# Matrix memory in steps of 64 tokens instead of 128, as 64x64 tiles of the array

## The chip, the cores and the metric

The kernel runs on one core of one Trainium2 chip. The time is the device time of one execution, in microseconds; three runs of the kernel before took 416.53, 416.6 and 417.84 us, so its median is 416.6 us. Profiles come from one further profiled execution. Engines are named as in the profile: PE is TensorE (matrix products; PEld its weight loads), DVE is VectorE, ACT is ScalarE, POOL is GpSimd, SP is SyncE, which issues the loads and stores.

## The reference

Two blocks follow each other. The first is a matrix-memory LSTM cell over q, k, v of shape 4 batches x 8 heads x 768 tokens x 40, with an input, a forget and an output gate:

```
m_new  = max(f[t] + m, i[t])
f_stab = exp(f[t] + m - m_new);  i_stab = exp(i[t] - m_new)
C = f_stab * C + i_stab * outer(v[t], k[t])        # 40 x 40 per head
n = f_stab * n + i_stab * k[t]
y[t] = sigmoid(o[t]) * (C q[t]) / max(|n . q[t]|, 1)
```

The heads are then put side by side (320 features a token). The second block takes the real part of a two-dimensional Fourier transform over tokens and features, adds it to its input, normalizes each token, and runs an MLP 320 -> 1280 -> 320 with a ReLU and a residual. All of it is float32.

## The kernel before

**The recurrence in chunks.** The 768 tokens of a batch are cut into NT = 6 chunks of L = 128. A chunk's output has two parts. One comes from the state C that entered the chunk: `mlstm_from_state` multiplies C by the queries, which `mlstm_scale_q` has scaled by their decay (`qg`). The other comes from the chunk itself: `mlstm_scores` makes k by q products (`ps`), `mlstm_exp` on ACT makes the weights W from the spread gate maxima, `mlstm_mask` on POOL zeroes the later tokens (batch 0 has the mask in its spread maxima), `mlstm_weigh` on DVE multiplies `ps` into W, and `mlstm_from_chunk` multiplies W by the values. Both parts add up in the PSUM tile `ph`. The values have a column of ones, so that n rides along as column 41 (D1).

The state goes on by `mlstm_to_state`: k times the weighted values `vw` (made by `mlstm_scale_v` on POOL) into `pc`. `mlstm_decay` on POOL multiplies the old state by the chunk's decay. In batch 0 the decayed state is added to `pc` by an identity product (L501) and ACT copies `pc` out (L511); in batches 1 to 3 DVE adds it (L515).

**Tiles of the array today.** Two heads share one set of operands. Scores (L465): two row tiles of 64 rows (40 in use) by 128 columns. State products (L479): C is block diagonal, two heads in one 128x128 product. Values (L486) and products to the state (L496): two column tiles, 128 rows by 64 columns. A score tile is the full 128x128 square, of which the upper triangle is used.

**After the products.** `mlstm_gather` (ACT) copies `ph` to `hT`, partly backwards, and moves the first column of a chunk to its neighbour; `mlstm_turn` transposes on TensorE into `px`; `mlstm_finish` (DVE, five operations, L549 to L555) divides, applies the output gate and writes x.

**Order.** There is no scheduler at work: `at(slot, phase, fn)` puts every piece of work into a plan by hand, and it is issued in that order on each engine's queue. Within a slot the phases are EVAC, FILL, MAIN and FILL_PE. Slots 0 to 31 have batch 0's recurrence, its Fourier products and the conversion of the MLP weights on DVE (`Piece`: the lines 344 to 364). From slot 31 on each slot has one step of some batch's MLP as MAIN, and the next batch's recurrence, one chunk each three slots, in FILL and FILL_PE around it: batch 1's from slot 32, batch 2's from 50, batch 3's from 82. The MLP's products are L861, L852 and L986 for batch 0, L923, L928 and L1042 for the others.

The PSUM pools: `ps_s` two banks (scores), `ps_h` two buffers of one bank shared by `ph`, `pc`, `px` and early transposes, `ps_m` four banks for everything else.

Of the kernel before, what the change touches and what calls it, by code (L numbers as in the profile page):

```python
# [19 lines left out]
L = 128  # L20
NT = S // L
NP = H // 2
D1 = D + 1
# [27 lines left out]
def kernel(  # L51
# [28 lines left out]
    ps_h = pool("ps_h", 2, space=PSUM)  # L80
    ps_m = pool("ps_m", 1, space=PSUM)

    turn = iter("3210321032120312031230123012012301023130201320132013201320123021320321")
# [11 lines left out]
    later_b = const.tile([L, L], BF, name="later_b")  # L95
    spread_sb = const.tile([BH, L + BH // 2], FP, name="spread_sb")
    colT = const.tile([L, NT, 2, BH], FP, name="colT")
    decB = const.tile([L, BH // 2, NT], FP, name="decB")
# [11 lines left out]
    C_bufs = [const.tile([L, NP, L], FP, name=f"C{n}") for n in range(3)]  # L110
# [3 lines left out]
    Cd_bufs = [s_last[:, n * NP * D1:(n + 1) * NP * D1].rearrange("p (n m) -> p n m", m=D1) for n in range(2)]  # L114
    hT_bufs = [const.tile([L, NP, L], FP, name=f"h{n}") for n in range(2)]
    M_d = dram.tile([NT, BH, L], FP, name="M_d")
    G_d = dram.tile([NT, 2, BH // 2, L], FP, name="G_d")
# [16 lines left out]
    def idle_products(n, first=False):  # L134
        pw = bank("pi", [L, 2 * L]) if first else ps_s.tile([L, 2 * L], FP, name="pi", tag="ps")
        for i in range(n):
            nc.tensor.matmul(pw, rest[:, 0:L], rest, start=True, stop=True, skip_group_check=True)


    def gates(gp):  # L140
        f_sb = gp.tile([BH, NT, L], FP, name="f_sb")
        a = gp.tile([BH, NT, L], FP, name="a")
        nc.sync.dma_start(out=f_sb.rearrange("p c t -> p (c t)"), in_=f_gate.rearrange("b h s -> (b h) s"))
        nc.sync.dma_start(out=a.rearrange("p c t -> p (c t)"), in_=i_gate.rearrange("b h s -> (b h) s"))
        keep = gp.tile([BH, NT, L], FP, name="keep")
        shift = gp.tile([BH, NT, L], FP, name="shift")
        m_in = gp.tile([BH, NT, 1], FP, name="m_in")
        F = gp.tile([BH, NT, L], FP, name="F")
        M = gp.tile([L, NT, L], FP, name="M")
        wk = gp.tile([BH, NT, L], FP, name="wk")  # L150
        g = gp.tile([L, NT, L], FP, name="g")
        nM = gp.tile([BH, NT], FP, name="nM")
        M3 = gp.tile([3 * BH, NT, L], BF, name="M3")
        below = gp.tile([BH, NT, L], BF, name="below")
        sel = gp.tile([3 * BH, BH], BF, name="sel")
        nc.vector.memset(rest, 0.0)
# [7 lines left out]
        nc.gpsimd.affine_select(out=later_b, in_=later_b, compare_op=OP.is_ge, fill=-M_INIT, base=0, pattern=[[1, L]],  # L164
                                channel_multiplier=-1)
# [6 lines left out]
        nc.vector.memset(M[:, 0:2], 0.0)  # L172
        for t in C_bufs:
            nc.scalar.copy(out=t.rearrange("p (two n) t -> p two (n t)", two=2),
                           in_=rest.unsqueeze(1).to_broadcast([L, 2, 2 * L]))
        nc.gpsimd.memset(qk_bufs[1][:, 0], 0.0)
        mlstm_load_o(0, 0)
        mlstm_load(0, 1)
        nc.gpsimd.memset(qk_bufs[2][:, 0], 0.0)
# [4 lines left out]
        for t in hT_bufs + Cd_bufs:  # L184
            nc.gpsimd.memset(t, 0.0)
# [8 lines left out]
        def maxima(s, initial):  # L194
            c0, c1 = s.start, s.stop
            nc.vector.tensor_tensor(out=a[:, s], in0=a[:, s], in1=F[:, s], op=OP.subtract)
            if c0 > 0:
                nc.vector.tensor_copy(out=shift[:, s, 0:1], in_=F[:, c0 - 1:c1 - 1, L - 1:L])
            nc.vector.tensor_tensor_scan(out=flat(M, s), data0=flat(shift, s), data1=flat(a, s), initial=initial,
                                         op0=OP.add, op1=OP.max)  # L200
            nc.vector.tensor_scalar(out=nM[:, s], in0=M[0:BH, s, L - 1], scalar1=-1.0, scalar2=None, op0=OP.mult)
            if c0 > 0:
                nc.vector.tensor_tensor(out=m_in[:, s], in0=M[0:BH, c0 - 1:c1 - 1, L - 1:L],
                                        in1=F[:, c0 - 1:c1 - 1, L - 1:L], op=OP.add)

        def spread_max(b, c, h0):

            k = chunks[b, c]
            if h0 == 0:
                k.W = wp.tile([L, H, L], FP, name="W", tag="W")  # L210
                k.M = []
            k.M.append(bank("pM", [L, NP, L]))
            nc.tensor.matmul(k.M[-1], ident_b, later_b.unsqueeze(1).to_broadcast([L, NP, L]), start=True, stop=False,
                             skip_group_check=True)
            for h in range(h0, h0 + NP):
                bh = b * H + h
                w, x = (ident[:, bh:bh + 1], M[:, c, :]) if c < 2 else (sel[:, bh:bh + 1], M3[:, c, :])
                nc.tensor.matmul(k.M[-1][:, h - h0, :], w.to_broadcast([w.shape[0], L]), x, start=False, stop=True,
                                 skip_group_check=True)
# [10 lines left out]
        def spread_decay(b, c):  # L230
            k = chunks[b, c]
            k.G = bank("pG", [L, NP, L])
            for h in range(H):
                r, bh = slice(h % 2 * 64, (h % 2 + 1) * 64), b * H + h
                nc.tensor.matmul(k.G[r, h // 2, :], ident[:, bh:bh + 1].to_broadcast([L, 64]), g[:, c, :],
                                 start=True, stop=True)

        def weights(s):
            for c in range(s.start, s.stop):
                nc.scalar.activation(out=wk[:, c], in_=a[:, c], func=AF.Exp, bias=nM[:, c:c + 1])  # L240
# [5 lines left out]
        def columns(s, j):  # L246
            pt = ps_h.tile([L, NT, BH], FP, name="pt", tag="ph")
            for c in range(s.start, s.stop):
                nc.tensor.transpose(pt[:, c, :], (a, wk)[j][:, c, :], ident[0:BH, 0:BH])
            return pt  # L250

        first, others, last = slice(0, 1), slice(1, NT), slice(2, NT)
        sums(first)
        maxima(first, M_INIT)
        pt = columns(first, 0)
        nc.scalar.copy(out=colT[:, first, 0], in_=pt[:, first])
        weights(first)
        spread_max(0, 0, 0)
        pt = columns(first, 1)
        spread_max(0, 0, NP)  # L260
# [3 lines left out]
        nc.vector.tensor_copy(out=colT[:, first, 1], in_=pt[:, first])  # L264
        mlstm_exp(0, 0, NP)
        maxima(others, M[0:BH, 0, L - 1:L])
        pt = columns(others, 0)
        mlstm_load_o(0, 1)
        nc.vector.memset(g[:, 1:3], 0.0)
        nc.vector.tensor_copy(out=colT[:, others, 0], in_=pt[:, others])  # L270
        decay(slice(1, 2))
        weights(others)
        spread_max(0, 1, 0)
        spread_max(0, 1, NP)
        spread_decay(0, 1)
        pt = columns(others, 1)
        late = {"pt": pt}
# [4 lines left out]

        def columns_late():
            nc.vector.tensor_copy(out=colT[:, others, 1], in_=late["pt"][:, others])

        def decay_late():
            decay(last)
            for hip in range(2):
                nc.sync.dma_start(out=G_d[1:NT, hip].rearrange("c p t -> p c t"), in_=g[hip:BH:2, 1:NT])

        def decays():
            dec = gp.tile([BH, BH // 2, NT], FP, name="dec")
            nc.vector.tensor_tensor(out=dec[:, :, 1:],
                                    in0=g[0:BH, 1:, L - 1].unsqueeze(1).to_broadcast([BH, BH // 2, NT - 1]),
# [983 lines left out]
```

## Time and profile before

| | |
|---|---|
| median of 3 runs | 416.6 us |
| profiled execution, first to last instruction (its span) | 414.0 us |
| median over this span | 2.6 us |
| granted TensorE clock | 1.000 |
| instructions | 8020 |
| PE, DVE, ACT, POOL busy | 404.0, 289.3, 188.8, 115.7 us |
| moved by DMA | 47.14 MB, mean 114 GB/s |
| first product of the MLP starts at | 57.4 us |

The page gives no time for the profiled execution other than its span; the 2.6 us are taken to lie around it. A float32 product stands in the trace as two weight loads and two products (`x16` in the chain is eight products). [...] In the rows of windows the columns are the stretch, its length, the busy time of PE, PEld, DVE, ACT and POOL with the number of instructions, the granted clock, the DMA engines' share and GB/s.

### The profile page before, as it was taken

The page shows a single profiled execution, that of the slowest core. Times are in us where ns is not written, and L with a number is a line of the kernel's source. Part 1 is how long each engine was busy: PE and PEld are TensorE (multiplying, and loading weights), DVE is VectorE, ACT ScalarE, POOL GpSimd, SP SyncE. Part 2 cuts the span into 40 slices and gives each one's busy share as a digit, 9 for nine tenths or more (in the row PEclk, how much of TensorE's full clock was granted, in tenths as well). Part 3 has the DMA queues.
Part 4 walks back from the last instruction along what each step waited for, and adds up shares of the span by engine and source line. Part 5 has one row for each costly group of instructions (what it writes and reads, how often), then busy time and mean ns, then how long its engine had stood idle before and what let it go on. Part 6 is the DMA issues. An engine that isn't in the chain of part 4 may idle for free.

```text
span 414.0 us, 8020 instructions
## 1 busy us (share of the span) xinstructions
PE 404.0 (98%) x2966; PEld 304.2 (73%) x2966; DVE 289.3 (70%) x682; ACT 188.8 (46%) x493; POOL 115.7 (28%) x194
## 2 busy tenths in 40 slices
PE   8999999999999999999999999999999999999997
PEld 6877555666667778776559998976559988555996
DVE  8789894978885548777874569787863786335652
ACT  6986366686651232655455413745551113355000
POOL 5554201567442420342061430342040000020000
PEclk9999999999999999999999999999999999999999
DMA  7899298479564154266100544310000000000010
GB/s 227 291 251 334 71 275 265 132 223 289 187 193 148 61 153 143 63 213 205 45 0 2 156 152 132 95 50 1 0 2 0 33 32 34 0 0 2 22 43 32
DMA packets 20549, 47.14 MB, mean 114 GB/s; under 512 B 2784, under 2 KB 9312, under 8 KB 20384
## 3 DMA queue, kind: packets, MB, share of 16 engines
q1 hardware_dynamic: 20512, 46.65, 36.6%
q8 instruction: 23, 0.38, 0.4%
q14 instruction: 14, 0.11, 0.1%
HBM read 42.52 MB, written 4.11 MB: 113 GB/s over the span
## 4 chain that ended last, share of the span: by engine, by line
PE 88%; DVE 8%; ACT 2%; POOL 1%; issue 1%; ACTq 0%; DVEq 0%
PE po L1042 18%; PE pm L923 17%; PE po L986 8%; PE pm L928 6%; PE ph L486 5%; PE pm L861 5%; PE ps L465 5%; PE ph L479 4%; PE pu L740 3%; PE px L540 2%; PE pm L852 2%; PE pz L709 2%; PE put L783 2%; PE pc L496 1%; PE pz L697 1%; DVE stats L767 1%
## 5 line engine op out<-in xcount | busy, mean ns | idle before, releaser
L992 DVE SCALAR_TENSOR_TENSOR x<-po,rstd,x 128x160 f32<-128x160 f32 (+1 forms) x69 | 27.0, 394 | 41.1 <-PE po L1042 35.5
L932 DVE TENSOR_TENSOR h<-h,pm 128x384 f32<-128x384 f32 x60 | 30.6, 550 | 30.4 <-PE pm L928 17.4
L421 ACT ACTIVATE W<-W,colT 128x128 f32<-128x128 f32 x144 | 45.1, 395 | 0.0
L443 POOL TENSOR_SCALAR_AFFINE_SELECT W<-W 128x1024 f32<-128x1024 f32 x18 | 22.4, 1247 | 75.4 <-ACT W L421 54.5
L923 PE MATMUL pm<-uT,w_sb 128*128 128x384 f32 x90 | 37.5, 504 | 0.2 <-DVE uT L911 0.2
L986 PE MATMUL po<-w_sb,h 128*128 128x320 f32 x120 | 34.4, 435 | 0.0
L471 DVE TENSOR_TENSOR W<-ps,W 128x512 f32<-128x512 f32 x48 | 30.7, 681 | 2.6 <-POOL W L443 2.3
L861 PE MATMUL pm<-uT,w_sb 128*128 128x384 f32 x80 | 29.7, 498 | 0.1
L986 PEld LDWEIGHTS po<-w_sb,h 128*128 128x128 f32 x120 | 22.3, 190 | 9.4 <-issue 0.8
L1042 PE MATMUL po<-T,S 128*128 128x160 f32 x180 | 27.9, 302 | 0.3 <-DVE x L992 0.3
L788 ACT COPY uT<-put 128x384 f32<-128x384 f32 x24 | 11.2, 478 | 37.1 <-PE put L783 37.1
L465 PE MATMUL ps<-qk 40*128 40x128 f32 x384 | 27.4, 282 | 0.0
L465 PEld LDWEIGHTS ps<-qk 40*128 40x128 f32 x384 | 23.9, 188 | 4.6 <-issue 0.7
L1042 PEld LDWEIGHTS po<-T,S 128*128 128x128 f32 x180 | 25.5, 190 | 1.7 <-DVE x L992 0.5
L1042 PE MATMUL po<-w_sb,h 128*128 128x160 f32 x180 | 26.5, 302 | 0.0
L524 ACT COPY h<-ph 41x512 f32<-41x512 f32 (+1 forms) x16 | 9.3, 582 | 37.1 <-PE ph L486 37.0
L1042 PEld LDWEIGHTS po<-w_sb,h 128*128 128x128 f32 x180 | 25.2, 190 | 1.3 <-DVE x L992 0.3
L431 POOL TENSOR_TENSOR qg<-qk,Gb 128x512 f32<-128x512 f32 x18 | 26.1, 1449 | 0.1
L486 PE MATMUL ph<-W,kvt 128*41 128x128 f32 x384 | 25.8, 277 | 0.0
L923 PEld LDWEIGHTS pm<-uT,w_sb 128*128 128x128 f32 x90 | 15.4, 190 | 13.2 <-DVE h L932 6.0
L479 PEld LDWEIGHTS ph<-qg,C 128*128 128x128 f32 x160 | 20.2, 192 | 5.5 <-POOL qg L431 1.6
L979 ACT ACTIVATE h<-h 128x384 f32<-128x384 f32 x45 | 23.1, 521 | 2.0 <-DVE h L932 2.0
(207 smaller groups left out, 844.5 us busy)
## 6 DMA issues: line engine op xcount, KB each, us to landing
W<-M_d SPq DMA_DIRECT2D x18, 512.0 KB
kvt<-in_kv SPq DMA_DIRECT2D x24, 324.0 KB
qk<-in_qkT SPq DMA_DIRECT2D x48, 160.0 KB
raw<-in_w SPq DMA_DIRECT2D x10, 640.0 KB
Gb<-G_d SPq DMA_DIRECT2D x36, 128.0 KB
so<-in_o SPq DMA_DIRECT2D x24, 160.0 KB
out<-x SPq DMA_DIRECT2D x24, 160.0 KB
ds_sb<-in_dft_s SPq DMA_DIRECT2D x1, 1155.0 KB
```

The source lines that it names most:

```text
L421: nc.scalar.activation(out=k.W[:, h, :], in_=M, func=AF.Exp, scale=-1.0, bias=colT[:, c, 0, b * H + h:b * H + h + 1])
L431: nc.gpsimd.tensor_tensor(out=k.qg, in0=k.qk[:, 0], in1=k.Gb, op=OP.mult)
L465: nc.tensor.matmul(k.ps[hip][:, p, :], k.qk[r, 1, p, :], k.qk[r, 0, p, :], start=True, stop=True)
L471: nc.vector.tensor_tensor(out=Wv, in0=k.ps[hip], in1=Wv, op=OP.mult)
L479: nc.tensor.matmul(k.ph[:, p, :], k.C[:, p, :], k.qg[:, p, :], start=(p == 0), stop=False, skip_group_check=True)
L486: nc.tensor.matmul(k.ph[hip * 64:hip * 64 + D1, p, :], k.v1[:, 2 * p + hip, :], k.W[:, 2 * p + hip, :], start=(c == 0 and p == 0), stop=Tr ...
L861: nc.tensor.matmul(k.pm[i], w1_sb[:, ch, f0:f0 + L], u[2 * ch], start=(ch == 0 and not ahead), stop=(ch == 1 and ahead), skip_group_check= ...
L923: nc.tensor.matmul(bank, w, u, start=start, stop=True, skip_group_check=True)
L932: nc.vector.tensor_tensor(out=h, in0=h, in1=bank, op=OP.add)
L986: nc.tensor.matmul(k.po, hidden(gr, f)[:, i * L:(i + 1) * L], w2_sb[:, f, :], start=(f == 0), stop=(f == NFF - 1))
L992: nc.vector.scalar_tensor_tensor(out=u, in0=po, scalar=k.rstd[:, c:c + 1], in1=u, op0=OP.mult, op1=OP.add)
L1042: nc.tensor.matmul(po, a[:, f], w[:, f], start=start and f == 0, stop=f == half - 1, skip_group_check=True)
```

## The change

The state is carried every LH = 64 tokens, in NS = 12 steps a batch; a chunk of 128 tokens stays the unit of the plan, and has two halves i = 0, 1.

- Scores are made only for the two 64x64 squares on the diagonal; W is 128 x 8 x 64. A query of the second half reaches the first half through the state.
- `mlstm_scores`, `mlstm_to_state`, `mlstm_from_state` and `mlstm_from_chunk` each issue 16 products of 64 (or 41) columns with at most 64 rows and 64 columns of weights, in an order (`TILES`) in which four neighbours stand in four tiles of the array. The two row tiles write different PSUM banks.
- In `mlstm_from_chunk` row tile i writes bank i ^ turn: the products are parted into turns 0 and 1, and between them `mlstm_between`, a copy of one element of `ph` by ACT, has to have run.
- `pc` goes into the score banks. The state is six buffers of 128 x 4 x 41; `mlstm_decay` (POOL, all 128 partitions) and `mlstm_state` (DVE, two operations of 40 x 164) run twice a chunk, in batch 0 too. The identity product and ACT's copies of `pc` go.
- `ps_h` has one buffer of two banks; `mlstm_gather` copies two times 41 partitions; `px` of batches 1 to 3 shares the buffer with `ph`, and `mlstm_turn` and `mlstm_finish` have new slots.
- The gates' maxima, decays and their spreading (batch 0: products L213, L218, L235) go by 64 tokens; the late decays and weights are subtracted on DVE (`sub_late`) and raised to exponentials in two ACT operations.
- Heads are paired as h and h + 4 instead of h and h + 1.

```
-    ps_h = pool("ps_h", 2, space=PSUM)
+    ps_h = pool("ps_h", 1, space=PSUM)
...
+            k.M = bank("pM", [L, H, LH], (0, 1, 1, 2, 1, 1)[c])
+            for i in range(2):
+                r = slice(i * LH, (i + 1) * LH)
+                nc.tensor.matmul(k.M[r], ident_b[:, r], later_b.unsqueeze(1).to_broadcast([L, H, LH]), start=True,
+                                 stop=False, skip_group_check=True)
...
+        def sub_late():
+            n = NS - last.start
+            nc.vector.tensor_tensor(out=g[0:BH, last], in0=m_in[:, last].to_broadcast([BH, n, LH]), in1=M[0:BH, last],
+                                    op=OP.subtract)
+            nc.vector.tensor_tensor(out=wk[:, last], in0=a[:, last], in1=nM[:, last].to_broadcast([BH, n, LH]), op=OP.add)
...
+        for i in range(2):
+            nc.sync.dma_start(out=k.W[i * LH:(i + 1) * LH],
+                              in_=M_d[c, i, b * H:(b + 1) * H, :].unsqueeze(0).to_broadcast([LH, H, LH]))
...
+    def mlstm_decay(b, c, i):
+        k, n = chunks[b, c], 2 * c + i
+        if 0 < n < NS - 1:
+            nc.gpsimd.tensor_tensor(out=k.C[i + 1], in0=k.C[i],
+                                    in1=decB[:, b * NP:(b + 1) * NP, n].unsqueeze(2).to_broadcast([L, NP, D1]), op=OP.mult)
+
+    def mlstm_state(b, c, i):
+        k, n = chunks[b, c], 2 * c + i
+        for r in (slice(0, D), slice(LH, LH + D)) if n < NS - 1 else ():
+            if n == 0:
+                nc.vector.tensor_copy(out=k.C[1][r], in_=k.pc[0][r])
+            else:
+                nc.vector.tensor_tensor(out=k.C[i + 1][r], in0=k.C[i + 1][r], in1=k.pc[i][r], op=OP.add)
+
+    TILES = ((0, 0), (1, 1), (0, 1), (1, 0))
+
+    def mlstm_scores(b, c):
+        ps = [ps_s.tile([L, NP * (LH + D1)], FP, name=f"ps{hip}", tag="ps") for hip in range(2)]
...
+        for p in range(NP):
+            for hip, i in TILES:
+                r, t = slice(hip * 64, hip * 64 + D), slice(i * LH, (i + 1) * LH)
+                product(k.ps[hip][t, p, :], k.qk[r, 1, p, t], k.qk[r, 0, p, t], True)
+
+    def mlstm_to_state(b, c):
+        k = chunks[b, c]
+        for p in range(NP):
+            for i, hip in TILES:
+                if 2 * c + i < NS - 1:
+                    r, h = slice(i * LH, (i + 1) * LH), hip * NP + p
+                    product(k.pc[i][hip * 64:hip * 64 + D, p, :], k.kn[r, h, :], k.vw[r, h, :], True)
...
+        for m in range(2):
+            for i in range(2):
+                for hip, side in TILES:
+                    if 2 * c + i > 0:
+                        r, t, p = slice(hip * 64, hip * 64 + D), slice(i * LH, (i + 1) * LH), 2 * m + side
+                        product(k.ph[side * 64:side * 64 + D1, hip, m, t], k.C[i][r, p, :], k.qg[r, p, t],
+                                m == 0 and i == (c == 0))
+
+    def mlstm_from_chunk(b, c, turn):
+        k = chunks[b, c]
+        for m in range(2):
+            for i, side in TILES:
+                hip = i ^ turn
+                r, h = slice(i * LH, (i + 1) * LH), hip * NP + 2 * m + side
+                product(k.ph[side * 64:side * 64 + D1, hip, m, r], k.v1[r, h, :], k.W[r, h, :], False)
+
+    def mlstm_between(b, c):
+        nc.scalar.copy(out=warm[0:1], in_=chunks[b, c].ph[0:1, 1, 1, L - 1:L])
...
+        for r in sides:
+            if c in BACKWARDS:
+                nc.scalar.copy(out=heads(k.hT)[r, :, :, 1:], in_=backwards(k.ph[r], L - 1, L - 1))
             else:
+                nc.scalar.copy(out=heads(k.hT)[r], in_=k.ph[r])
...
+            for i in range(2):
+                if b == 0 and c < 2:
+                    d, t = (((1, 0), (1, FILL - 0.2)), ((3, FILL - 0.1), (4, FILL - 0.3)), ((4, FILL - 0.25), (4, FILL + 0.55)),
+                            ((5, FILL + 0.05), (5, FILL + 0.4)))[2 * c + i]
+                else:
+                    d, t = (s + i, FILL + 0.05), (s + 1 + i, FILL - 0.2)
+                at(*d, mlstm_decay, b, c, i)
+                at(*t, mlstm_state, b, c, i)
...
+            ahead = b > 0 and end
+            at(s + 3, MAIN - 0.1 if ahead else FILL_PE, mlstm_from_state, b, c)
+            at(s + 3, MAIN - 0.1 if ahead else FILL_PE, mlstm_from_chunk, b, c, 0)
+            at(s + 3, MAIN if ahead else FILL_PE + 0.5, mlstm_between, b, c)
+            at(s + 3, FILL_PE + 3, mlstm_from_chunk, b, c, 1)
+            at(s + 4, FILL, mlstm_gather, b, c)
...
+                t = s0 + (8, 11, 14, 17, 20, 20)[c]
+                x = t + end
+                at(t, MAIN - 0.1, mlstm_turn, b, c)
+            at(x, FILL + 0.05 if b == 0 or end else MAIN + 0.55, mlstm_finish, b, c)
```

## The prediction

> **What bounds the kernel now.** I read the busy shares first, then the chain of work that ended last, then the groups by line, then the windows by stage.
>
> ```profile
> PE 404.0 (98%) x2966; PEld 304.2 (73%) x2966; DVE 289.3 (70%) x682; ACT 188.8 (46%) x493; POOL 115.7 (28%) x194
> DVE  8789894978885548777874569787863786335652
> ```
>
> PE (TensorE) is busy 98% of the span, and DVE (VectorE) is near 90% in the first slices: two engines to watch, not one.
>
> ```profile
> PE 88%; DVE 8%; ACT 2%; POOL 1%; issue 1%; ACTq 0%; DVEq 0%
> ```
>
> The chain agrees: TensorE's own products set the end. What a product costs shows in a piece of that chain (start, length, what):
>
> ```profile
> 18.06 1.09 PE ph L479 x8
> 19.15 1.09 PE ps L465 x16
> 20.24 1.00 PE ph L486 x16
> 21.24 0.31 PE pc L496 x16
> 21.55 0.30 PE pc L501 x4
> ...
> 21.88 0.29 ACT C L511
> ```
>
> Every float32 product is two records. Within such a run, starts on one tile of the array are 109 ns apart for 128 columns, 136 for 160 (L1042), 269 for 320 (L986) and 322 for 384 (L923): 0.833 ns a column plus 2.5 ns. L465 has two row tiles and L486 two column tiles at work at once, so their 16 records take the time of 8. L496 keeps the rule for 41 columns: 37 ns a tile, two tiles, 16 records in 0.31 us, 19 ns a record. By this rule all records together need 369.5 us of the 414.0; the other 44.5 us are waits (mostly before 57 us) and changes of tile shape: from the last scores to the first values product 147 ns more than the rule, from `pc` to the next full-array product 113 ns.
>
> The stages, cut at the MLP's own products (us; PE, PEld, DVE, ACT, POOL busy):
>
> ```profile
> 0.00:57.45 57.45, 52.39 (x536) 39.50 (x536) 49.54 (x106) 39.49 (x113) 24.82 (x49) 1.00 0.77 240
> 57.45:119.94 62.49, 61.30 (x488) 40.76 (x488) 49.62 (x100) 41.06 (x108) 30.11 (x41) 1.00 0.74 220
> 119.94:178.47 58.53, 58.53 (x419) 44.14 (x417) 38.53 (x94) 21.06 (x60) 17.86 (x21) 1.00 0.40 124
> 218.36:271.32 52.96, 52.90 (x504) 49.51 (x502) 37.88 (x100) 21.40 (x61) 17.53 (x21) 1.00 0.37 114
> ```
>
> The first stage has batch 0's six chunks and no MLP; in it DVE has nearly no room:
>
> ```profile
> 13.00:30.00 17.00, 15.78 (x230) 13.13 (x227) 14.77 (x25) 15.22 (x47) 8.43 (x18) 1.00 0.88 266
> 30.00:48.04 18.04, 16.42 (x187) 12.34 (x186) 16.36 (x45) 8.77 (x27) 8.05 (x12) 1.00 0.70 233
> ```
>
> 31.1 of these 35.0 us are DVE work, and of the 3.9 idle ones I find about 3.5 in waits for PE, POOL and ACT. The last 104 us hold no recurrent work and stay.
>
> **TensorE, part by part.** For a middle chunk today: state products 8 records x 109 = 0.87 us, scores 16/2 x 109 = 0.87, values 0.87, products to the state 16/2 x 37 = 0.29; 2.9 us. After: 32 records for each of the four; with four tiles at once 32/4 x 56 (64 columns: 0.833 x 64 + 2.5) = 0.45 for the first three and 32/4 x 37 = 0.29 for the last; 1.64 us. Four at once is not in this trace. The nearest rows are two row tiles (L465) and two column tiles (L486, L496), each working at full rate, so I take full rate; the other end is that only two run at once, 112 ns for four records. Over 24 chunks, with the first and last chunks' missing products and batch 0's L501: 66.4 us become 37.7, or 75.4 at the other end.
>
> The gate spreading of batch 0 halves too (64 columns, two column tiles): L213 2.6 to 1.3 us, L218 5.3 to 2.7, plus 0.45 for the first chunk's decay: -3.4. By stage, the need falls by 11.2, 7.9, 3.6, 2.4, 4.5 and 2.3 us: 31.9 in all. Scores, `mlstm_to_state` and both kinds of values product now have one tile shape, so the 147 ns change goes: 18 chunks beside the MLP, -2.6 us; bounds 0 and -4.
>
> [...]
>
> **What else rides on it.** DVE, per chunk: the two `mlstm_weigh` products shrink from 512 to 256 columns; L471 (681 ns) against L515 (321 ns for 164) is 1.03 ns a column, so 0.26 less each, -0.53. The state now is updated twice a chunk, 4 operations of L515's kind (321 ns, starts 335 apart): 1.3 us, against 0.65 today for batches 1 to 3 and none for batch 0, whose copies were ACT's (L511). So +0.1 a chunk later, +0.8 in batch 0. In the first stage also `sub_late`'s two 32x512 operations (L196 takes 0.73 for 640: 0.6 each) and the first chunk's `qg` (0.33): together 12 x -0.26 + 22 x 0.33 + 1.2 + 0.3 + some 0.3 of small copies = +5.9 us on an engine with 3.9 to spare. Moreover chunks 2, 3 and 4 of batch 0 have their two state updates back to back on DVE, and the second waits for `mlstm_decay` on POOL (L455: 0.46 to 0.57), which waits for the first: about 0.7 us of standing DVE each, +2.1; all of batch 0's finishing is queued behind. Of today's waits on PE, POOL and ACT I let 2.9 go. First stage: +5 us although TensorE needs 11 less; bounds -3 (all idle absorbed, stalls hidden) and +9 (nothing absorbed, more stalls).
>
> ACT: exponentials of 64 columns are shorter (0.836 ns a column between L788's and L524's copies, -0.05 each), gather becomes two 41-partition copies (L524, 0.58 each: +0.58), first columns two of 0.17, and `mlstm_between` one more small copy, bound by L528's 0.17. ACT is busy 46%: nothing, if it doesn't come late. It matters at one place: `mlstm_from_chunk(…, 1)` waits for `mlstm_between`, and the MLP's products queue behind it on PE. The cover is the scores and to-state products between, 0.45 + 0.29 = 0.74 us, against a product's 0.28 to its end plus 0.17; hidden. If ACT is still in its four exponentials (4 x 0.31), up to 0.5 us a chunk shows: 0 to 9 us over 18 chunks; I take 0. POOL: the mask in two pieces of 512 columns costs what one of 1024 does (L443, 1.25); decays stay two a chunk. SP issues twice as many loads for `W`, half as large (L401, 0.35 us each), far ahead of use: nothing. `ps_h` has one buffer: `px` must be finished (L549 to L555, 1.55 us of DVE) before the next `ph`; a main step of about 3 us (62.5 us for 20 slots) stands between. Uncovered it would cost 1.5 us a chunk.
>
> **The sum**, against the profiled execution: first stage +5; second -6 of 7.9, since DVE's 49.6 (+0.7 for states, -2.0 for a finish that moves on) would fill 88% of a stage 7.9 shorter, and it must wait for PE in places; then -3.4, -2.3, -4.2, -2.1 (a tenth left to waits); tile shape -2.6; last 104 us 0. That is -15.6: 414.0 becomes 398.4. The median lies 2.6 above this span, so 401.0.
>
> **Rivals.** (a) *DVE has room after all*: the first stage keeps its time, the other five give all their 20.7, shape -3.5: -24, 392 us. For it: today's chain there is mostly PE. Against it: 31.1 of 35. (b) *DVE and POOL bind harder*: first stage +9, second -3, then -9.5, shape -2.6: -6, 411 us. For it: the alternating DVE/POOL chain. (c) *Four tiles give no more than two*: TensorE's need beside the MLP rises by 6.8 instead of falling; with shape -2.6 and first stage +6, 427 us, slower. Place: each group of four records; it decides from about 91 ns for four (23 a record), where +5 - 2.6 and the gain cancel; 56 is what the rows of two tiles give. (d) *Instructions come late*: the trace shows 23 fetches of 16 KB on queue q8, about 1.04 us each, and 23 x 256 is TensorE's count of instructions; some 14 more are needed, and a burst of 128 records now passes 256 instructions in 1.6 us. If each of 18 chunks waits one fetch, the gain is gone: 419 us. Against it: no "issue" of that size today.
>
> **How the numbers follow.** Forecast (395 to 406) 0.44; (a) 0.20; (b) 0.19; (c) 0.12; (d) 0.05. Within 0.3% (1.25 us, what a measurement here can tell) falls little of (b) and (d): 0.03. Faster 0.83, slower 0.14. The range 386 to 417 takes in (a), (b) and the forecast and leaves out (c), most of (d) and a tail below.
>
> **What would show it.** Right: runs of 32 records with starts some 56 ns apart by four, 0.45 us for scores where 1.09 stood; MLP start after 57.4, not before, with DVE the chain there; the stage to the first `po` about 56 us; the last 104 us unchanged. Wrong: scores of 0.9 us or more (c), PE waiting for ACT's small copy each chunk, or an MLP start before 55 us (a).

## The result: slower, and the profile after

Measured: 433.2 us (median of 4 runs, 430.4 to 436.8) against 417.1 us before (416.5 to 417.8, runs beside it): ratio 1.040, 95% interval 1.033 to 1.046. The forecast was 401. The profiled execution took 431.4 us, its span 429.7: a time lies 1.7 us above its span here and in the runs below, not 2.6. Medians and ranges take in every execution; ratios leave out those more than 1.5% above the fastest of their kernel.

The page of the changed kernel, first busy time, share and instructions of each engine, then two rows of the 40 slices (10.7 us each):

```profile
PE 394.5 (92%) x4728; PEld 284.1 (66%) x4728; DVE 293.1 (68%) x747; ACT 193.4 (45%) x538; POOL 125.3 (29%) x228
DVE  8785777197796865877686578785775586435562
PEclk9785579998999999999999999999999999999999
```

TensorE fell from 98% of the span to 92%, on a longer span. DVE did not fill up: its first slices are emptier than before. What is new is the third row. Before it was 9 throughout; now the granted clock of TensorE falls to about half near 20 us and from 32 to 60 us.

Its chain of work that ended last, by engine:

```profile
PE 64%; issue 12%; DVE 12%; DMA 5%; POOL 4%; ACT 1%; SPq 0%; POOLq 0%; DVEq 0%; ACTq 0%
```

88% of the chain was TensorE's before; now 36% of it stands on other engines and on transfers, and a third of that is "issue", time for which no engine or semaphore is to blame.

The stages, cut at the MLP's products as before (us; PE, PEld, DVE, ACT, POOL busy, then clock, DMA share, GB/s):

```profile
0.00:71.89 71.89, 55.90 (x1025) 41.00 (x1025) 53.77 (x135) 37.37 (x113) 27.87 (x53) 0.74 0.66 198
71.89:138.09 66.20, 56.94 (x956) 33.45 (x956) 47.47 (x106) 41.75 (x119) 31.72 (x51) 0.97 0.58 172
138.09:191.93 53.84, 53.84 (x706) 39.26 (x701) 37.88 (x106) 21.64 (x69) 18.10 (x27) 1.00 0.39 114
191.93:234.46 42.53, 40.50 (x371) 22.47 (x366) 31.02 (x80) 24.72 (x67) 14.49 (x30) 1.00 0.30 82
```

Against before: first stage 71.9 for 57.4 (+14.4), second 66.2 for 62.5 (+3.7), third 53.8 for 58.5 (-4.7), fourth 42.5 for 39.9 (+2.6), then 51.2 for 53.0 (-1.8) and 39.7 for 38.3 (+1.4). The last 104.4 us are as before. Together +15.7: the whole difference of the two spans.

The products themselves do what was forecast. A piece of the chain (start, length, what):

```profile
147.30 0.59 PE ph L495 x32
147.90 0.78 PE ps L495 x64
148.67 0.23 PE ph L495 x16
148.90 2.89 PE po L1040 x10
```

Scores and products to the state, 64 records, take 0.78 us (forecast 0.45 + 0.29); starts come by four, 56 to 58 ns apart (37 for 41 columns), and no gap stands between one kind of product and the next. By the forecast's rule (0.833 ns a column, four tiles at full rate) all records need 337.5 us instead of 369.5: 32 us less work, and 16 us more time.

Windows of 3.41 us of the first stage (in this trace one granted clock holds for 10.24, 10.24, 6.83, 27.31, 40.96 and 3.41 us up to 104 us: whole multiples of 3.41), chosen around the clock's changes (columns as above; the clock is the third number from the end):

```profile
12.09:15.50 3.41, 2.29 (x52) 1.62 (x48) 2.53 (x6) 1.08 (x7) 2.83 (x4) 1.00 1.01 335
15.51:18.91 3.40, 1.16 (x49) 1.16 (x53) 3.14 (x8) 1.20 (x3) 1.38 (x2) 0.50 0.64 221
29.17:32.56 3.39, 1.94 (x110) 1.47 (x99) 3.31 (x7) 2.73 (x11) 1.27 (x4) 1.00 0.83 259
32.58:35.97 3.39, 1.53 (x27) 1.00 (x27) 2.56 (x11) 1.31 (x3) 2.53 (x4) 0.50 0.02 9
56.47:59.87 3.40, 3.40 (x11) 1.85 (x10) 3.05 (x10) 0.00 (x0) 0.62 (x1) 0.50 0.00 0
59.89:63.28 3.39, 3.39 (x13) 1.56 (x12) 3.05 (x5) 0.01 (x1) 0.00 (x0) 1.00 0.28 48
```

In 12.09 to 15.50 the records need only 0.34 of the window at full rate (PE shows 2.29 us busy: a record lasts 0.2 to 0.3 us, while the next on its tile can start 0.06 us after it); the next window runs at half clock. The same at 29.17. At half clock the products took twice as long (four records of the values every 107 ns instead of 56). From 32.58 on TensorE still stands in every window waiting for others (busy for 94% at most), and the clock stays down for 27.3 us, until a window is full from end to end (56.47).

Three further waits (the timeline of the changed kernel: start, length, engine, line, operation, tiles; in brackets the idle time before it and what ended it). The first two are SyncE issuing loads, the third is DVE:

```profile
68.89 1.10 SPq L426 DMA_DIRECT2D W<-M_d  x2
80.14 1.09 SPq L435 DMA_DIRECT2D Gb<-G_d  x2
```

```profile
86.31 0.49 DVE L369 TENSOR_SCALAR e<-raw 128x640 uint32<-128x640 uint32 x1 [9.02 <-DMA raw<-in_w]
```

Between the two loads SyncE stands for 10 us: the load of `Gb` waits for one of two buffers, and the raw weights (`raw`, the MLP's weights ahead of their conversion on DVE) queued behind it land late. DVE waits 9 us for them, with the weighing of the scores queued behind, and TensorE 2.95 us for that.

```profile
31.46 0.31 PE L495 MATMUL ph<-W,kvt 64*41 64x64 f32 x6
34.05 0.54 PE L495 MATMUL ph<-W,kvt 64*41 64x64 f32 x9 [2.29 <-issue]
205.90 0.66 PE L495 MATMUL ph<-qg,C 40*41 40x64 f32 x32 [1.19 <-DVE x L597]
```

At 31.8 TensorE stops in the middle of a run of equal products, with nothing to wait for; the "issue" of the chain. At 204.7 the last chunk's `ph` waits for the finish of `px`, which has the one `ps_h` buffer.

One more loss stands in no wait. The MLP's products with 64 rows come in pairs on two row tiles, with starts 7 ns apart. Their rows before, then after (line, engine, operation, tiles, shape, count, then busy us and the mean ns of one):

```profile
L928 PE MATMUL pm<-uT,w1t_sb 64*128 64x384 f32 x120 | 23.9, 509 | 0.0
```

```profile
L982 PE MATMUL pm<-uT,w1t_sb 64*128 64x384 f32 x120 | 27.3, 513 | 0.0
```

The same products fill 3.4 us more, 1.9 in the fourth stage and 1.5 in the sixth. Some pairs came apart there: the second record of a pair starts after the first one's columns, 0.32 or 0.43 us later, and a weight load there often starts 0.05 us after DVE's addition (L986) or ACT's copy (L1018) has ended.

### The profile page after: what moved, and what is told of

Same layout as the page of the kernel before. It is cut to its first block, busy times and chain, and to the rows that moved or that the text cites. A ratio compares the mean times of both kernels' runs of the same rounds, so it can differ in the third digit from the quotient of the medians.

```text
span 429.7 us, 11757 instructions
## 1 busy us (share of the span) xinstructions
PE 394.5 (92%) x4728; PEld 284.1 (66%) x4728; DVE 293.1 (68%) x747; ACT 193.4 (45%) x538; POOL 125.3 (29%) x228
## 4 chain that ended last, share of the span: by engine, by line
PE 64%; issue 12%; DVE 12%; DMA 5%; POOL 4%; ACT 1%; SPq 0%; POOLq 0%; DVEq 0%; ACTq 0%
PE po L1096 18%; PE pm L977 14%; PE po L1040 8%; PE pm L982 5%; PE ph L495 5%; PE ps L495 3%; DMA raw<-in_w 2%; PE px L582 2%; PE pu L794 2%; DVE C L488 2%; PE pm L915 2%; DMA so<-in_o 2%; POOL W L471 1%; DVE W L520 1%; PE pz L751 1%
## 5 line engine op out<-in xcount | busy, mean ns | idle before, releaser
L471 POOL TENSOR_SCALAR_AFFINE_SELECT W<-W 64x512 f32<-64x512 f32 x36 | 25.1, 698 | 90.0 <-ACT W L450 88.8
L986 DVE TENSOR_TENSOR h<-h,pm 128x384 f32<-128x384 f32 x60 | 30.7, 550 | 29.9 <-PE pm L977 17.0
L450 ACT ACTIVATE W<-W,colT 128x64 f32<-128x64 f32 x144 | 38.1, 338 | 0.0
L488 DVE TENSOR_TENSOR C<-C,ps 40x164 f32<-40x164 f32 x80 | 25.6, 320 | 17.4 <-POOL C L478 10.3
L495 PE MATMUL ph<-W,kvt 64*41 64x64 f32 x768 | 24.1, 235 | 8.5 <-DVE W L520 6.1
L478 POOL TENSOR_TENSOR C<-C,decB 128x164 f32<-128x164 f32 x40 | 20.7, 518 | 33.6 <-DVE C L488 29.3
L546 ACT COPY warm<-ph 1x1 f32<-1x1 f32 x24 | 3.5, 147 | 59.8 <-PE ph L495 59.8
L982 PE MATMUL pm<-uT,w1t_sb 64*128 64x384 f32 x120 | 27.3, 513 | 0.0
L1096 PE MATMUL po<-w_sb,h 128*128 128x160 f32 x180 | 26.6, 301 | 0.0
L460 POOL TENSOR_TENSOR qg<-qk,Gb 128x512 f32<-128x512 f32 (+1 forms) x21 | 26.2, 1250 | 0.4
L495 PEld LDWEIGHTS ph<-W,kvt 64*41 64x41 f32 x768 | 17.1, 126 | 11.5 <-DVE W L520 7.4
L495 PEld LDWEIGHTS ph<-qg,C 40*41 40x41 f32 x704 | 12.9, 126 | 16.2 <-issue 9.6
```

Source lines behind the costliest of these rows:

```text
L450: nc.scalar.activation(out=k.W[:, h, :], in_=(k.M if b == 0 else k.W)[:, h, :], func=AF.Exp, scale=-1.0, bias=colT[:, c, 0, b * H + h:b * ...
L460: nc.gpsimd.tensor_tensor(out=k.qg[:, :, t], in0=k.qk[:, 0, :, t], in1=k.Gb[:, :, t], op=OP.mult)
L471: nc.gpsimd.affine_select(out=W, in_=W, compare_op=OP.is_ge, fill=0.0, base=0, pattern=[[0, H], [1, LH]], channel_multiplier=-1)
L488: nc.vector.tensor_tensor(out=k.C[i + 1][r], in0=k.C[i + 1][r], in1=k.pc[i][r], op=OP.add)
L495: return nc.tensor.matmul(out, w, x, start=start, stop=True, skip_group_check=True)
L982: nc.tensor.matmul(bank, block(w1t_sb, i)[rows], mlp_u(gr, 1)[rows], start=False, stop=True, skip_group_check=True)
```

## Experiments: clock, queue, buffer, late instructions

Theory: the first stage lost its time to the half clock and the second to SyncE's queue. Rival: the chain of DVE and POOL paces both, and the half clock only fills time that TensorE would have stood anyway.

### One: idle products, a third buffer

```diff
 # e1: into the 92 unused columns of the score banks, batch 0
+    for i in range(n):
+        nc.tensor.matmul(chunks[0, c].tail[i % 2], rest[:, 0:L], rest[:, 0:4 * L - NP * (LH + D1)], start=True, ...)
+    at(..., FILL_PE + 2.04, keep_busy, c - 1, 5)     # ahead of scores
+    at(s + 3, FILL_PE - 0.01, keep_busy, ..., 5)     # ahead of from_state
 # e2
-    k.Gb = gbp.tile([L, NP, L], FP, name="Gb", tag="Gb")
+    k.Gb = gbp.tile([L, NP, L], FP, name="Gb", tag="Gb", bufs=3)
 # e3: e1 and e2.   e4: e3 and
-    ahead = b > 0 and end
+    ahead = False
```

e1, idle products:

> Products of zeros (128x128 by 92 columns, two records, about 0.16 us at full clock) into the unused 92 columns of the score banks: five ahead of each chunk's scores and five ahead of each chunk's from_state in batch 0, some 55 in all, 8.7 us of TensorE work that nobody reads. Theory (clock): in the first 72 us the profile of the changed kernel shows the granted clock at 0.5 for 37.5 us, always after a 3.4 us window in which the records' need was 0.34 of the window or less; the work done in those stretches needs 12.7 us at full clock and took twice that. Expected: clock 0.9 or more in the first stage, MLP start at 59 to 65 us instead of 71.9, time 7 to 13 us less than the changed kernel (420 to 426 us). Rival (alternating DVE and POOL chain): the half clock only fills time that TensorE would have stood; clock back at 1.0, MLP start within 3 us of 71.9 or later, time 431 to 436.

Measured: 434.0 us (427.7 to 436.6), ratio 1.034 (1.025 to 1.042). In the profiled execution, the slowest of the four, the MLP started at 77.3, with clock 0.87 in the first stage. The theory's gain did not come. But the products were a bad tool: records of 92 columns started 112 ns apart where their columns need 79 (with weights of the same 128x128, records of 128 columns start 112 ns apart in the kernel before, L218, and records of 256 columns 218, L137), and five products stood 1.28 us on the chain itself in one place (at 24.3 us). What the executions tell is something else: 427.7 us at a mean clock of 0.995, 433.3 at 0.976. Within one kernel clock and time go together; which moves which, this run can't say.

e2, the third buffer:

> A third buffer for the decay rows Gb, nothing else. Theory (queue of loads): chunk 0 of a batch now loads Gb too; with two buffers its successor's load stands in SP's queue for some 10 us near 70 to 80 us, and the raw weight words behind it land 9 us late, which holds DVE, and TensorE waits 2.95 and 2.23 us for DVE W and then gets half clock for 3.4 us. Expected: the 9 us wait of L369 for the transfer gone, second stage 66.2 to 59-62 us, time 4 to 8 us less than the changed kernel (425 to 429). Rival (DVE and POOL bind the second stage anyway): wait gone, stage 64 us or more, time within 2 us of 433.

Measured: 424.3 us (424.0 to 428.2), ratio 1.021 (1.016 to 1.026): 9 us less than the changed kernel. Second stage:

```profile
70.50:131.70 61.20, 56.51 (x956) 33.30 (x956) 48.63 (x106) 41.55 (x119) 32.21 (x51) 0.97 0.65 192
```

66.2 became 61.2 and the longest wait for the raw weights 2.1 us. Shown: SyncE's queue cost 5.0 us there. (The three other runs with two buffers, e1, e10 and e14, have 66.3 to 68.5 in this stage, the ten others with three 60.7 to 64.8.)

e3 and e4:

> Both edits: the idle products of batch 0 and the third Gb buffer. Theory (both causes, separate stages): the gains add, 12 to 20 us less than the changed kernel, 413 to 421 us, MLP start 59 to 65 us, first product to the output about 119 to 126 us. Rival (DVE and POOL chain in both stages): 428 us or more. A third reading (the queue only matters because the first stage is late): gain no more than with the idle products alone.

> Both edits, and the last chunk of batches 1 to 3 no longer ahead of the MLP's products: its from_state, first half of from_chunk and the small copy go behind them as for the other chunks. In the changed kernel its first product waits 1.16 us twice for the finish of px, which shares the one buffer ps_h. Theory (shared buffer): those waits go, 1 to 3 us less than both edits alone. Rival (the small copy on ACT is then uncovered, since no scores follow the last chunk): its 0.3 to 0.5 us a batch eats most of it, within 1 us of both edits alone.

Measured: 424.6 (421.9 to 428.5) and 424.8 us (420.6 to 434.0); ratios 1.017 (1.011 to 1.024) and 1.017 (1.011 to 1.023). In e3 the gains did not add: 8.6 us less than the changed kernel instead of 12 to 20, MLP start 73.9. In time e4 decides nothing, its executions lie too far apart (420.6 to 425.9 us at clocks from 0.991 to 0.976). By stage it does; the fourth stage of e3, then of e4:

```profile
189.00:231.50 42.50, 40.47 (x370) 22.44 (x367) 31.02 (x80) 24.68 (x66) 14.47 (x30) 1.00 0.33 93
```

```profile
184.90:226.40 41.50, 40.34 (x376) 22.51 (x367) 31.02 (x80) 24.89 (x67) 14.46 (x30) 1.00 0.33 96
```

At the products' own starts it is 1.1 us less (42.54, 41.43), and the sixth stage 1.1 less (39.66, 38.56). The shared buffer cost about 2 us. But e4's first stage, at clock 0.98, was still 69.8 us: a point for the rival, or for the idle products' own cost.

### Two: denser idle products, DVE's order, no decay

```diff
 # e5: e2, e4's edit, and 17 products of 256 columns into the spare half of the ph banks
+    nc.tensor.matmul(chunks[0, c].spare, rest[:, 0:L], rest, start=True, stop=True, ...)
 # e6: e2 and the first raw weights' DVE operations behind chunk 0's second state update
-    when = [((2, 0.7), (4, 0.5), (6, 0.6)), ...
+    when = [((4, -0.28), (4, 0.5), (6, 0.6)), ...
 # e7: e5 and e6.   e8: e7 without mlstm_decay's nc.gpsimd.tensor_tensor
```

The products of e5, e7 and e8 start a new sum in the bank in which h is being summed, and batch 0's h is not the reference's in these three; they are read for their times alone.

> The idle work made cheap: zeros 128x128 by 256 columns (0.43 us a product, no column of it wasted on loading weights) into the spare half of the ph banks, 17 products in batch 0 instead of 55 small ones: three ahead of chunk 1's scores, two ahead of each later chunk's, one ahead of each px. With it the third Gb buffer and the last chunk not ahead. Earlier runs: the 55 small ones kept the clock but stood on the path themselves, 1.3 us in each of 11 places; over single executions of one kernel, time grew by 0.6 to 0.74 us for each us of clock lost. Theory (half clock is the larger part of the first stage's loss, the small products hid it by their own cost): clock 0.99, MLP start 60 to 66 us, time 410 to 417. Rival (the chain of DVE and POOL sets the first stage whatever the clock): MLP start 68 us or more, time 418 to 424.

> Third Gb buffer, and the first two DVE operations on the raw weights (1.3 us) moved behind chunk 0's second state update on DVE. No idle products. In the changed kernel chunk 1's scores stand 3.07 us at 14.7 us for that update, since scores and products to the state share a bank, and the half clock follows. Theory (the shared bank makes the scores wait for DVE's queue, and that wait starts the half clock): the wait falls to 1 to 1.8 us, the first stretch of half clock goes or moves, and the time falls 2 to 6 us under the third Gb buffer alone (418 to 422). Rival (the records are too thin wherever the wait is): the half clock comes all the same, time 422 to 428.

> All of it: cheap idle products, third Gb buffer, last chunk not ahead, raw weights behind the state update. Theory (separate causes, both hold): 1 to 2 us less than without the move, 408 to 416, that is even with or below the kernel before. Rival (first stage set by DVE and POOL): 417 to 423, the move worth less than 1 us.

> As the run with all of it, and the state's decay on POOL left out (10 of 11 operations a batch: the state is added to old contents of its buffer, so this part of the computation is missing): the state updates of a chunk wait for POOL no more. Theory of the forecast (the alternating chain of DVE and POOL costs some 0.7 us of standing DVE in three chunks of batch 0): MLP start 2 to 4 us earlier than with the decay, little after it. Rival (other work covers it): within 1 us.

Measured: e5 423.1 us (422.8 to 425.6), e6 424.2 (423.2 to 427.1), e7 423.6 (419.9 to 431.2), e8 424.4 (420.6 to 431.5); ratios 1.016 (1.012 to 1.020), 1.019 (1.014 to 1.024), 1.013 (1.007 to 1.019), 1.018 (1.009 to 1.027). Nowhere did the theory get its 408 to 417. e5 had clock 1.00 in its first stage and MLP start at 68.6 all the same. Its chain says why:

```profile
23.34 0.03 ACT warm L551
...
23.41 1.13 PE ph L510 x4
24.54 0.93 PE ps L495 x62
```

The idle products (L510) wait for ACT's small copy out of their bank, and the scores queue behind them: a wait that the changed kernel doesn't have. Again the probe was on the path. e6 moved the state update, and the wait for it fell from 3.07 to 1.73 us, but the half clock came all the same (clock 0.76 in the first stage, MLP start 70.3 against e2's 70.5): its rival was right. e8 against e7: MLP start 71.2 against 69.6, at the same clock of 0.93. Of this, e8 stood 2.1 us in "issue" gaps, e7 0.2; without them the two lie 0.3 us apart. Leaving POOL's decay out brought 2 to 4 us nowhere, so the alternation of DVE and POOL is mostly covered by other work.

### Three: idle products that hold nothing up

```diff
 # e9: e6, e4's edit, and in mlstm_turn, batch 0
     k.px = bank("px", [L, NP, L], (3, 0, 2, 3, 1, 2)[c])
+    keep_busy(k.px, 2)                               # 256 columns each, overwritten by the transposes
+    at(3, FILL_PE + 2.04, lambda: keep_busy(bank("pi", [L, NP, L], 3), 4))
 # e10: the changed kernel and, in batch 0
-    k.ph = ps_h.tile([L, 2, 2, 2, L], ...)[:, :, 0]
+    k.ph = k.both[:, :, c % 2 if b == 0 else 0]      # one tile for the batch, halves in turn
 # e11: e9 and e10
```

> Third Gb buffer, last chunk not ahead, raw weights behind the state update, and idle products of 256 columns (0.43 us each) only where they can't hold anything up: two into each px bank of batch 0 just ahead of its transposes, which wait for ACT there anyway, and four into a free bank ahead of chunk 1's scores. The earlier idle products took the clock to 0.99 but stood on the path themselves or waited for readers of the bank they wrote to; the Fourier part of batch 0 began at 54 to 56 us in every run so far, 43.4 in the kernel before. Theory (half clock is most of the first stage's loss): clock 0.98 or more, Fourier part at 46 to 51 us, time 407 to 413, faster than the kernel before. Rival (a chain through the single ph buffer, ACT's gather and small copy, and DVE sets batch 0's pace): Fourier part at 53 us or later, time 417 to 422.

> The changed kernel with one edit: in batch 0 the chunks take the two halves of the ph banks in turn, so that a chunk's from_state need not wait for ACT's gather of the chunk before. Theory (the single buffer paces batch 0): Fourier part 3 to 8 us earlier than 55.9, time 425 to 430. Rival (half clock or DVE paces it): within 1.5 us of the changed kernel, 431 to 435.

> Both: the cheap idle products with their three fixes, and ph in turn in batch 0. Theory (clock and buffer each cost): 2 to 6 us less than without the halves in turn. Rival (one of them covers the other): within 1 us of it.

Measured: e9 419.8 us (417.5 to 425.3, 8 runs), ratio 1.008 (1.005 to 1.011). e6 and e9 differ in the first stage only in the idle products; e6, then e9:

```profile
0.00:70.30 70.30, 55.25 (x1026) 40.42 (x1026) 53.32 (x135) 37.25 (x113) 27.46 (x53) 0.76 0.68 203
```

```profile
0.00:64.90 64.90, 52.45 (x1058) 37.99 (x1058) 53.61 (x135) 37.30 (x113) 27.94 (x53) 1.00 0.72 211
```

More products, 5.4 us less: the clock went from 0.76 to 1.00. (Net: e9's first stage also stood 4.9 us in "issue" gaps, e6's 2.8.) Between e9's executions too: 417.5 us at clock 0.992, 422.6 at 0.980. The Fourier part began at 50.8 us, inside the theory's 46 to 51 (the earlier runs had it at 53.9 to 61.6, not 54 to 56), but the time fell in the rival's 417 to 422: half clock was part of the loss. e10: 429.6 us (429.1 to 432.1), 1.033 (1.029 to 1.037); the Fourier part 3.0 us earlier than the changed kernel's 55.9, at the near edge of its theory, some of it lost again in the second stage (68.5). With the clock up the halves in turn bring nothing in time: e11 419.3 (416.7 to 421.4), 1.007 (1.004 to 1.011).

### Four: what was left

In e9's first stage, too, TensorE stops with nothing to wait for: 2.15 us at 23.4, 1.17 at 29.2, 1.58 at 34.7. Counting TensorE's instructions (products, weight loads and semaphore instructions) in order, 34 of the 35 "issue" gaps of 0.3 us or more ahead of a product in all 16 profiles stand ahead of number 256n + 193 and end 1.25 to 1.6 us after a 16 KB transfer of queue q8 has landed (the other, 2.01 us in e10, stands ahead of scores that have a semaphore to wait for; the kernel before has no such gap). Three runs asked what this is, whether the clock counts by itself, and whether DVE's order is the rest.

```diff
 # e12: e9 and, at the start
+    for i in range(32):
+        nc.tensor.matmul(pw[0:64, 0:8], rest[0:64, 0:64], rest[0:64, 0:8], start=True, stop=True, ...)
 # e13: e9 and chunk 1's mlstm_finish later
-    t, x = ((8, 11), (11, 14), ...
+    t, x = ((8, 11), (11, 17), ...
 # e14: the changed kernel and e9's idle products alone
```

> As the run with the idle products in the px banks, and 32 products of 8 columns more at the very start, beside the three idle ones there, where TensorE waits for the gates anyway: 128 more instructions on TensorE (two records and two weight loads a product), no work moved. In all profiles so far TensorE's gaps that no semaphore explains stand ahead of instructions 961, 1217, 1473, 3777, 4033 or 7361 of TensorE's count, each 193 more than a multiple of 256, and end 1.25 to 1.5 us after a 16 KB transfer of queue q8 has landed; the kernel before has none. Theory (TensorE runs into instructions that are not there yet): the gaps stay ahead of instructions 256n + 193 (the count includes the new ones), that is, in other places of the code, half a block earlier; total gap time 2 to 8 us; time within 2 us of 419.8. Rival (they belong to those places in the code): gaps at 1089, 1345, 1601.

> As the run with the idle products in the px banks, and chunk 1's finish (five DVE operations, 1.5 us) three slots later in batch 0. There three finishes stand back to back on DVE from 39.7 to 44.7 us, and chunk 5's weigh and state update behind them; TensorE waits 1.77 us for that state. Theory (order on DVE): that wait falls to 0.3 us or less, Fourier part 1 to 1.7 us earlier (49 to 50), time 1 to 2 us less (418 to 419). Rival (ACT's gather ends as late): within 0.5 us.

> The changed kernel with one edit: the idle products (two into each px bank of batch 0 ahead of its transposes, four into a free bank ahead of chunk 1's scores; 16 of 0.43 us). Theory (half clock): clock 0.5 for no more than 10 us of the first stage instead of 37.5, MLP start at 65 to 67 us instead of 71.9, time 5 to 7 us less than the changed kernel (426 to 428). Rival (the other edits of the run before made the difference): MLP start within 2 us of 71.9, time 431 to 434.

e12: 425.5 us (423.4 to 426.6), 1.021 (1.017 to 1.026). The time missed its expectation: the 64 small records took 7.0 us, 109 ns each, and the first transpose of the gates, queued behind them, began at 11.0 us instead of e9's 4.1. The place did not. Its timeline:

```profile
48.97 0.42 PE L497 MATMUL ph<-W,kvt 64*41 64x64 f32 x12
51.26 0.31 PE L497 MATMUL ph<-W,kvt 64*41 64x64 f32 x4 [1.87 <-issue]
```

This gap, the only one in e12 (1.87 us, under the 2 to 8 expected in all), is ahead of number 1985 = 7 x 256 + 193, which without the 128 new instructions is 1857; no other run stopped there, and none of 1089, 1345 and 1601 had a gap. So the gap went with the count, not with the code, as the theory wanted; that instructions come late is read from this and from the landings on q8, whose transfers the page calls "instruction". (The counts 705 and 1729, in e8, e1 and e2, were missing from the list in the expectation; they fit the rule too.)

e13: 420.6 us (417.3 to 421.6), 1.008 (1.004 to 1.012). DVE made chunk 5's state 1.2 us earlier, but the Fourier part began at 51.6 instead of 50.8: no gain. The expectation had misread the wait. In both runs TensorE stands 1.80 us ahead of chunk 5's products with the state, and ACT's gather of the chunk before ends it; only two stops within them, 0.4 us in all, went with the state. The rival was right. (A wait of 1.7 us at 7.5 us that e9 lacked hides up to that much.)

e14: 426.1 us (422.7 to 427.1), 1.021 (1.016 to 1.026), as the theory wanted: idle work alone takes 7 us off the changed kernel. Not all of it is the clock: of the 4.3 us that its profiled span is shorter, 2.9 lie in the first stage and 1.7 in the fifth, where the changed kernel's gap of 1.82 us ahead of instruction 7361 did not come. Its first stage:

```profile
0.00:69.00 69.00, 58.62 (x1057) 42.80 (x1057) 53.59 (x135) 37.27 (x113) 27.95 (x53) 0.88 0.67 199
```

Half clock still held for 17 us of it (10 were expected), and the MLP began at 69.0, not 65 to 67; the execution at clock 0.992 took 422.7.

No version beats the kernel before: e9, e11 and e13 lie 0.7 to 0.8% above it.

## Why the prediction was wrong, step by step

**TensorE's need, four tiles at once, one tile shape: right.** -31.9 us forecast, -32.0 by the same rule in the trace; 58 ns by four for 64 columns, 37 for 41. Rival (c) is refuted. Across the four tiles starts came 14.5 and 9 ns apart on average; on one tile they stayed 58 and 37 ns apart. The 147 ns between kinds of product are gone.

**First stage, +5 forecast, +14.4 measured: the step that failed most.** It was built on "DVE has nearly no room". DVE's added work was about right (49.5 to 53.8 us, +4.2 for +5.9), but DVE was busy only 75% of the longer stage, and of the 2.1 us of standing DVE for POOL's decay e8 shows 0.3 on the path. What was missing is what thinner work cost here: "TensorE needs 11 less" thinned its windows (to 0.34 at 12.09 and 29.17 us) until the clock fell to 0.50, and the remaining products took twice as long (107 ns for 56). The row for it stood in the forecast's own windows (clock 1.00 everywhere), and the working never asked what went with it: up to 140 us no window of 3.41 us in the kernel before needed less than 0.63 at full rate, in the changed kernel two needed 0.34 and the clock fell after each. Price, from e6 to e9: 5.4 us. At full clock the stage is still 7.5 us longer than before; 4.9 of that are late instructions if all of them lie on the path, which leaves 2.6 for what the forecast had priced at 5.

**Second stage, -6 forecast, +3.7 measured.** "SP issues twice as many loads ... nothing" looked at W, and never at chunk 0's new load of Gb, which takes a buffer from the next chunk and stops the queue: 5.0 us (e2). With it mended the stage is 61.2, 1.3 less than before; TensorE still waits 2.2 us there for weighed scores, and 1.4 for ACT's gather ahead of `px`.

**Fourth to sixth stage, -2.3, -4.2, -2.1 forecast; +2.6, -1.8, +1.4 measured.** The fourth stage before, for comparison:

```profile
178.47:218.36 39.89, 39.89 (x227) 24.65 (x223) 29.16 (x75) 21.73 (x55) 12.45 (x27) 1.00 0.35 106
```

"A main step of about 3 us ... stands between" is wrong for the last chunk of a batch, whose `ph` is put ahead of the MLP's products, straight behind `px`: 1.19 us in the fourth stage, and 1.1 each won back in the fourth and sixth in e4. That `px` itself now stands ahead of the MLP's products, and so waits for ACT's gather (idle for 0.54 and 0.19 us in the fourth stage), was not seen at all. Nor were the MLP's pairs that come apart, 1.9 us in the fourth and 1.5 in the sixth: the forecast counted the work of DVE and ACT there, not when the MLP gets their results. 27.3 us stand in this row in every run but e8 (26.6), so no experiment here took the loss away, and its cause is read from the trace alone. In the fifth stage the gap of 1.82 us for instructions is most of the 2.4 missing. The third stage (-3.4 forecast) gave -4.7.

**`mlstm_between` at nothing: right.** In the whole changed kernel no product waits 0.15 us or more for it. In e9, where the last chunk's copy has no scores to cover it, TensorE stood 0.33 us for it in the fourth stage.

**Rival (d), instructions late, 0.05.** 37 transfers were counted and 37 came. Not one in each chunk, but three gaps in the changed kernel (2.28, 0.53 and 1.82 us: 4.6) and five in e9 (7.6). 'No "issue" of that size today' was a poor argument: before, the fastest 256 instructions took 7.8 us, and now 1.7.

**The sum.** The span missed its forecast by 31.3 us (429.7 for 398.4). The causes priced by runs and gaps, 5.4 (clock) + 5.0 (queue) + 2.2 (buffer) + 4.6 (instructions) = 17.2, are a little more than half of that; with the pairs, read from the trace, it is 20.6. They don't strictly add, since a queue mended also moves the clock (e2 gained 9 us in time, 5.0 in its stage; e14 7 in time). The other third is open. One slip of the forecast's own is small: "a tenth left to waits" took 0.8 off the 12.8 us of four stages, a sixteenth. Not settled: why a transfer on q8 sometimes starts late (in the changed kernel at 31.4 us, 4.6 after TensorE had entered the block before it), and what keeps e9's second stage 6.7 us above the forecast; 2.7 of that are gaps for instructions.

## What to carry to other kernels

Here 32 us less work on the busiest engine became 16 us more time, part of it since what remained no longer filled its windows (0.34 of one, then clock 0.50): ask of each stage what its share of work will be afterwards, and look in the traces for the clock that windows like that had. An operation added for one chunk (here a load of Gb, 5.0 us in e2) goes through queues and buffers that the others use; follow it there even if it is far ahead of its own use. And place a probe that adds idle work where the engine waits anyway, in a bank that nobody reads: e1's stood 1.28 us on the chain in one place and e5's waited for ACT's copy, while e9's brought the first stage from 70.3 to 64.9 us.

## What the runs showed of the hardware

**In these profiles the clock fell after thin work, not only after idle time.** In 15 profiles (all but e12), between 4 and 140 us, the clock fell to half 39 times, 37 of them after a window of 3.41 us in which the records' need at full rate was 0.42 of the window or less; of windows with less than 0.40 only two kept it (0.35, 0.38). It came back only after a window in which TensorE was busy for 98% or more (39 of 39), though ten others just as full left it at half. In the changed kernel's 12.09 to 15.50 TensorE shows 67% busy, and the clock fell. Nor did "busy" alone raise it in e12: there TensorE shows 5.00 us busy of every 5.00 from 5 to 15 us, first with the small records, and the trace first records full clock at 19.8 us, against 5.3 in the changed kernel; the 32 records of `pM` at 17.57 us still took 1.92 us, in e9 at 10.14 us 1.15. What sets the clock is not shown beyond these counts.

**Gaps without a semaphore stand at steps of 256 in TensorE's count, after a transfer on q8.** The page's row for these transfers in the changed kernel:

```profile
q8 instruction: 37, 0.61, 0.6%
```

They are of 16 KB each, and their number is that of the places 256n + 193 in the count: 37 of 9553 instructions there, 23 of 6042 in the kernel before. That each brings 256 instructions, a block, is read from these numbers; no run shows it directly. 16 KB took 0.9 to 1.9 us on q8, and where TensorE stood at such a place, it went on 1.25 to 1.6 us after the landing. The recurrent part now issues 64 instructions for 32 records where 16 records needed 32, at a quarter of the time each (scores: starts 14.5 ns apart on average for 54.5). Speed alone did not bring a gap: the fastest 256 instructions of the changed kernel (1.7 us, at 190 us) have none. Ahead of the 34 gaps TensorE spent 2.0 to 6.9 us on the block before, less than the 7.8 us of any 256 instructions in the kernel before, and the transfer began 0.5 to 5.4 us after TensorE had entered that block. What delays its start is open.
